# Attention and MoE in one kernel: token rows of eight, one-hot matmuls for the global tokens, bias matmuls for the mask, and units of eight query blocks

## The chip, the cores and the metric

The kernel runs on one core of one Trainium2 chip. The metric is device time in microseconds (us). On one core a run is called slow when it is over 1.5% above the fastest run of the same kernel, and slow runs are left out of every ratio. Ratios below are the mean time of one kernel's fast runs over that of the other's of the same rounds, so they are not quite the ratio of the medians that are quoted.

The kernel before took 381.72 us, the median of three runs (380.2 to 382.25).

## The reference

```python
# batch 8, heads 8, sequence 576, head size 64; 8 global tokens, window 32
def _attn_ref(q, k, v, global_idx):
    scores = scale * np.matmul(q, k.transpose(0, 1, 3, 2))
    mask = np.abs(pos[:, None] - pos[None, :]) <= window
    mask = mask | is_global[:, None] | is_global[None, :]
    scores = np.where(mask, scores, -1000000000.0)
    ...                                   # softmax
    return np.matmul(attn, v)

# 4608 tokens, d_model 512, d_ff 2048
def _moe_ref(x, w_in, w_out, alpha):
    h = x @ w_in
    s = np.sin(alpha * h)
    g = h + s * s / (alpha + 1e-09)
    return g @ w_out
```

A query sees the keys within 32 positions and eight global keys. A global query sees all keys. The result of the attention is the input of the two layers. The comparison with the reference has a tolerance.

## The kernel before

Each batch has 12 blocks of 48 queries for each of four pairs of heads. A block sees 112 window keys and 8 global keys, and its 48 columns of queries are followed by 8 columns of global queries, so a block is 56 columns wide. A unit is six blocks. For each unit the tensor engine (PE) makes scores, ScalarE (ACT) the exponentials, VectorE (DVE) the mask product, PE the denominators and numerators, and DVE writes the result into `xT`, which is the transposed input of the first layer for all 4608 tokens. The matmuls of batch p-1's second layer are laid between the units of batch p's attention as filler, and then batch p's first layer follows.

The start of the kernel gathers the rows of the global tokens of all batches, 24 transfers with offsets that are read at run time, into tiles of their own:

```python
    gN = [setup.tile([NG * B, DM], F32, name=f"gN{i}") for i in range(3)]
    ...
    for i, src in enumerate((k, q, v)):
        for eng, js in halves:
            for j in js:
                eng.dma_start(
                    out=gN[i][j : NG * B : NG, :].rearrange("b (h d) -> b h d", d=D),
                    in_=src[:, :, bass.ds(regs[j], 1), :].rearrange("b h o d -> b h (o d)"),
                )
    ...
    # cast to bf16, transpose, and put into the global columns of qT and kTw,
    # and into the global rows of the value tile by a broadcast transfer:
    globals_all()
    globals_v_all()
    shift_v(0)
    global_v(0)
```

The layers and the tail of the attention:

```python
    # first layer of batch c (512 tokens; nine such, the last without attention ahead of it):
    # a 128-row slice of d_ff at a time
    for ci in range(CT):
        nc.tensor.matmul(out=h2[:], lhsT=w_in[:, ci, nt * P : (nt + 1) * P],
                         rhs=xT[:, ci, c * CH : (c + 1) * CH], ...)
    ...
    # end of a batch's attention: the columns of the eight global queries
    for j in range(NG):
        nc.gpsimd.tensor_copy(
            out=xT[:, :, b * S : (b + 1) * S][:, :, bass.ds(pregs[j], 1)],
            in_=xg[:, :, j : j + 1],
        )
```

The softmax here doesn't subtract the row's maximum and nothing guards it: scores larger than these inputs give would overflow.

## Time and profile before

The span of the profiled run is 378.6 us. I divide it at the starts of the first layers:

| piece of the span | us |
|---|---|
| from the start to the first layer of batch 0 | 46.60 |
| batch-1 period (to the first layer of batch 1) | 43.49 |
| batch-2 period | 38.12 |
| later periods, each | 38.0 |
| from the first layer of batch 2 to the end | 250.4 |

The page's second part shows the span in forty slices. A digit is the busy share of PE in tenths, and PEclk is the clock that was granted to it.

```profile
PE   1127499698999999999999999999999999999996
PEclk9999999999999999999999999999999999999999
```

From the eleventh slice on PE is at nine tenths: the kernel is bound by the tensor engine, except in the first five slices, which are 47 us. The timeline of PE shows what these consist of. The columns are start, duration, engine, source line, operation with output and inputs, shapes, count, and in brackets the idle time ahead of it with what ended it.

```profile
14.44 0.39 PE L268 MATMUL ops<-identb,gB 64*128 64x64 bf16 x4 [6.92 <-DVE gB L266]
...
19.76 0.46 PE L336 MATMUL Sp<-qT,kTw 64*128 64x56 bf16 x12
...
29.58 0.57 PE L375 MATMUL num<-E,VW 128*64 128x56 bf16 x12 [3.08 <-DMA VW<-VgN]
...
42.73 0.52 PE L375 MATMUL num<-E,VW 128*64 128x56 bf16 x12 [0.45 <-DVE gn L386]
46.60 0.59 PE L457 MATMUL hb<-xT,w_in 128*128 128x512 bf16 x1 [3.35 <-POOL xT L402]
...
90.09 9.67 PE L457 MATMUL hb<-xT,w_in 128*128 128x512 bf16 x43 [1.46 <-POOL xT L402]
...
128.21 9.66 PE L457 MATMUL hb<-xT,w_in 128*128 128x512 bf16 x43
```

The start is a chain of waits. The gathered rows come first (14.44), then scores (19.76), then the first numerator waits for the broadcast of the global values (29.58), then eight units follow to 42.73, and the copies on POOL (GpSimd) end the wait for the first layer at 46.60. The difference of two first-layer starts is a period. PE is little loaded up to the first numerator. The windows view gives, for 8 to 30 us, the length and then the busy time of PE, PEld (weight loads), DVE, ACT and POOL, the clock and the load of the DMA engines:

```profile
8.00:30.00 22.00, 4.20 (x72) 3.04 (x72) 11.60 (x37) 5.49 (x8) 14.97 (x22) 1.00 1.70 148
```

PE works for 4.20 of the 22 us. The copy of the keys out of PSUM is a unit-step copy, in the page's fifth part (busy, mean ns):

```profile
L310 DVE COPY kTw<-Kps 128x1344 bf16<-128x1344 bf16 x32 | 27.1, 848 | 1.9 <-PE Kps L304 1.9
```

### The profile page before, as it was taken

To read this page: it belongs to the slowest core of one execution; us is meant where nothing else is said; L and a number is where in the kernel's file an instruction comes from. 1 tells how busy PE (TensorE), PEld (TensorE's weight loads), DVE (VectorE), ACT (ScalarE), POOL (GpSimd) and SP (SyncE) were. 2 spreads that over 40 slices of the span, in tenths; PEclk is the share of its full clock that TensorE was granted. 3 is DMA by queue.
4 is the path that set the end of the run, shared out by engine and by line. 5 is a ranking of instruction groups with operands and counts; after the bars stand their busy time and mean duration, and the time that the engine had idled before them with its cause. 6 is when DMAs were issued, how large, how long until landed. Compare 5 with 4: busy or idle time off the path is not lost.

```text
span 378.6 us, 8594 instructions
## 1 busy us (share of the span) xinstructions
PE 328.3 (87%) x3173; PEld 164.0 (43%) x3224; DVE 244.5 (65%) x556; ACT 258.1 (68%) x435; POOL 245.6 (65%) x390
## 2 busy tenths in 40 slices
PE   1127499698999999999999999999999999999996
PEld 0015244343444444444444444445444544444444
DVE  7735459574987487748774877487748774866510
ACT  1056587795998588858885888588858885845411
POOL 8944297136979489948994899489948303965100
PEclk9999999999999999999999999999999999999999
DMA  6999999546999428951896289628962001000112
GB/s 52 131 167 168 192 156 162 56 51 90 156 135 164 103 40 74 164 109 45 70 165 110 47 64 167 110 51 62 169 100 58 29 32 55 2 1 28 55 57 83
DMA packets 133867, 35.31 MB, mean 93 GB/s; under 512 B 123330, under 2 KB 128450, under 8 KB 133826
## 3 DMA queue, kind: packets, MB, share of 16 engines
q0 software_dynamic: 122560, 19.02, 70.0%
q1 hardware_dynamic: 8034, 15.40, 14.1%
q10 hardware_dynamic: 3232, 0.34, 0.8%
q8 instruction: 25, 0.41, 0.5%
q14 instruction: 16, 0.13, 0.1%
HBM read 38.42 MB, written 9.44 MB: 126 GB/s over the span
## 4 chain that ended last, share of the span: by engine, by line
PE 53%; ACT 17%; POOL 10%; issue 8%; DVE 8%; DMA 2%; POOLq 1%; ACTq 0%; DVEq 0%
PE hb L457 22%; PE ops L494 12%; PE o L494 8%; ACT Sb L464 6%; ACT E L342 3%; PE num L375 3%; ACT S L470 2%; DVE H2b L447 2%; DMA KS<-in_k_dram 2%; DVE S L472 2%; DVE kTw L310 2%; PE hb L494 2%; PE Sp L336 2%; ACT lnd L358 2%; POOL QS L95 2%
## 5 line engine op out<-in xcount | busy, mean ns | idle before, releaser
L457 PE MATMUL hb<-xT,w_in 128*128 128x512 bf16 x562 | 130.7, 382 | 7.0 <-POOL xT L402 4.8
L464 ACT ACTIVATE Sb<-hb,alphaT 128x512 bf16<-128x512 f32 x144 | 96.6, 684 | 52.4 <-PE hb L457 51.1
L447 DVE SCALAR_TENSOR_TENSOR H2b<-S,recipT,hb 128x512 bf16<-128x512 bf16 x144 | 102.2, 740 | 21.0 <-POOL S L472 21.0
L472 POOL TENSOR_TENSOR S<-Sb 128x512 bf16<-128x512 bf16 x87 | 88.4, 1040 | 29.7 <-ACT Sb L464 29.5
L457 PEld LDWEIGHTS <-w_in 128*128 128x128 bf16 x576 | 56.4, 98 | 73.7 <-issue 9.5
L494 PE MATMUL ops<-w_out,H2b 128*128 128x512 bf16 x286 | 73.3, 380 | 2.3 <-issue 1.7
L494 PEld LDWEIGHTS <-H2b 128*128 128x128 bf16 x560 | 48.7, 98 | 52.6 <-issue 2.2
L344 DVE TENSOR_TENSOR E<-E,MASK 128x672 bf16<-128x672 bf16 x64 | 33.1, 519 | 32.8 <-ACT E L342 32.1
L494 PE MATMUL o<-w_out,H2b 128*128 128x512 bf16 x206 | 50.6, 379 | 2.2 <-issue 1.9
L342 ACT ACTIVATE E<-Sp 128x672 bf16<-128x672 f32 x64 | 45.9, 717 | 4.1 <-PE Sp L336 4.0
L402 POOL COPY xT<-xg 128x4 bf16 x64 | 12.9, 201 | 48.7 <-DVE xg L400 45.3
L107 POOL DMA_DIRECT2D VW<-in_v_dram x56 | 42.7, 796 | 0.4 <-issue 0.3
L358 ACT ACTIVATE lnd<-den 128x288 f32<-128x288 f32 x64 | 26.4, 412 | 17.7 <-PE den L352 17.2
L472 DVE TENSOR_TENSOR S<-Sb 128x512 bf16<-128x512 bf16 x35 | 20.4, 582 | 25.0 <-ACT Sb L464 24.1
L382 DVE TENSOR_TENSOR xT<-num,rec 128x288 bf16<-128x288 f32 x64 | 28.7, 448 | 6.8 <-PE num L375 5.4
L375 PEld LDWEIGHTS <-VW 128*64 128x64 bf16 x768 | 18.3, 116 | 32.6 <-DVE gn L386 10.2
L375 PE MATMUL num<-E,VW 128*64 128x56 bf16 x768 | 25.3, 201 | 6.6 <-DMA VW<-VgN 3.1
L360 ACT ACTIVATE rec<-lnd 128x288 f32<-128x288 f32 x64 | 28.3, 443 | 2.0
L310 DVE COPY kTw<-Kps 128x1344 bf16<-128x1344 bf16 x32 | 27.1, 848 | 1.9 <-PE Kps L304 1.9
L336 PE MATMUL Sp<-qT,kTw 64*128 64x56 bf16 x768 | 22.1, 190 | 6.0 <-ACT E L342 4.2
L100 POOL DMA_DIRECT2D QS<-in_q_dram x30 | 23.6, 786 | 2.8 <-DMA QS<-in_q_dram 2.8
L324 ACT COPY qT<-qp 128x576 bf16<-128x576 bf16 x20 | 12.6, 632 | 18.1 <-DMA gN<-in_v_dram 13.7
(77 smaller groups left out, 314.3 us busy)
## 6 DMA issues: line engine op xcount, KB each, us to landing
out_dram<-osb SPq DMA_DIRECT2D x35, 256.0 KB
VW<-in_v_dram POOLq DMA_DIRECT2D x40, 112.0 KB, 4.4
VW<-VW SPq DMA_DIRECT2D x8, 384.0 KB
KS<-in_k_dram POOLq DMA_DIRECT2D x30, 96.0 KB, 4.6
QS<-in_q_dram POOLq DMA_DIRECT2D x30, 96.0 KB, 4.6
w_in<-in_moe_w_in_dram POOLq DMA_DIRECT2D x4, 512.0 KB, 9.0
w_out<-in_moe_w_out_dram POOLq DMA_DIRECT2D x4, 512.0 KB, 13.7
VW<-VW SPq DMA_DIRECT2D x8, 240.0 KB
```

The costliest lines, as they stand in the source:

```text
L107: nc.gpsimd.dma_start(out=W[p0 : p0 + n, par, u, :].rearrange("p (h d) -> p h d", d=D), in_=v[b, :, key0 : key0 + n, :].rearrange("h p d - ...
L310: nc.vector.tensor_copy(out=kTw[hp][:, :, 0:KB], in_=bass.AP(tensor=base.tensor, offset=base.offset, ap=[list(base.ap[0]), [QB, NW], [1, KB]],
L336: nc.tensor.matmul(out=Sp[:, t, u * QC : (u + 1) * QC], lhsT=kTw[hp][pr, i, :], rhs=qT[hp][pr, i, :], start=True, stop=True, skip_group_ch ...
L342: nc.scalar.activation(out=E[:], in_=Sp[:, :, 0:EW], func=AF.Exp, scale=scale)
L344: nc.vector.tensor_tensor(out=E[:], in0=E[:], in1=mk[:, None, :].to_broadcast([P, 2, EW]), op=ALU.mult)
L358: nc.scalar.activation(out=lnd[:], in_=den[:, :, 0:QB], func=AF.Ln)
L375: nc.tensor.matmul(out=num[pr, u, :], lhsT=W[:, i % 2, i // 2, c0 : c0 + 64], rhs=E[:, t, u * QC : (u + 1) * QC], start=True, stop=True, s ...
L447: nc.vector.scalar_tensor_tensor(out=H2b[:, n_, :], in0=s_[:], scalar=recipT[:, n_ : n_ + 1], in1=h_, op0=ALU.mult, op1=ALU.add,)
L457: nc.tensor.matmul(out=h2[:], lhsT=w_in[:, ci, nt * P : (nt + 1) * P], rhs=xT[:, ci, c * CH : (c + 1) * CH], start=(ci == 0), stop=(ci == ...
L464: nc.scalar.activation(out=Sb[:], in_=h2[:], func=AF.Sin, scale=alphaT[:, nt : nt + 1])
L472: eng.tensor_tensor(out=S2[:], in0=Sb[:], in1=Sb[:], op=ALU.mult)
L494: nc.tensor.matmul(out=ops[:], lhsT=H2b[:, nt, ts * P : (ts + 1) * P], rhs=w_out[:, nt, :], start=(nt == 0), stop=(nt == NT - 1),)
```

## The change

The intent is to start without the gathers. For batches 0 and 1, q and k come in rows of eight tokens. The global rows of q, k and v of these two batches are picked by matmuls with one-hot matrices that the core makes from the indices. Batch 0 gets its mask as a bias, added to the scores by a matmul with the identity, so that ACT's exponentials are masked already. The 24 gathers are still needed for batches 2 and later, and are moved behind the start: twelve are issued after the first shift of v, twelve inside the first layer of batch 0. Their rows are put into a part of `xT` that the attention does not fill until batch 6. The one-hot matrices lie in another such part, that of batches 4 and 5. The unit becomes eight blocks, so there are six units per batch.

The diff, cut to its core (the address arithmetic of the transposes, the mask tables and the renamed arguments are left out):

```diff
+    NB = 8
...
+    late_x = slice(NTOK - 2 * DM, NTOK)
+    gN = [xT[0 : NG * B, i, late_x].bitcast(F32) for i in range(3)]
+    gB = [xT[0 : NG * B, 3, NTOK - (2 - i) * DM : NTOK - (1 - i) * DM] for i in range(2)]
...
-    gN = [setup.tile([NG * B, DM], F32, name=f"gN{i}") for i in range(3)]
-    halves = ((nc.sync, range(0, NG // 2)), (nc.scalar, range(NG // 2, NG)))
-    ...                                   # all 24 gathers in the setup
...
+    OHV = xT[:, 0, early_x : early_x + (NU + 1) * P].rearrange("p (a b) -> p a b", b=P)
+    VgZ = xT[:, 1, early_x : early_x + DM]
...
+    def globals_v(b):                     # global rows of v by one-hot matmuls
+        for u in range(NU):
+            nc.tensor.matmul(
+                out=vp[:], lhsT=OHV[0:KB, u, :], rhs=W[0:KB, 0, u, :], ...
+            )
+        ...
+        nc.vector.tensor_copy(out=VgZ, in_=vp[:])
...
+    def globals_hp(b, hp, pool, tag):     # global rows of q and k by one-hot matmuls
+        for i, src in enumerate((qk[b][1], qk[b][0])):
+            for j in range(R8):
+                for t, pr in heads:
+                    nc.tensor.matmul(
+                        out=gp[pr, i, :],
+                        lhsT=src[:, 2 * hp + t, j, :], rhs=OH[0:NP8, j, :], ...
+                    )
...
+        if b == 0:                        # the mask of batch 0
+            for t, pr in heads:
+                nc.tensor.matmul(
+                    out=Sp[:, t, 0:EW], lhsT=identb[:],
+                    rhs=BIAS[:, i0 : i0 + NB, :].rearrange("p u c -> p (u c)"),
+                    start=True, stop=False, ...
+                )
...
-            nc.gpsimd.tensor_copy(
+            copy, r = nc.gpsimd.tensor_copy, pregs
+            if b == 0 and j % 2:
+                copy, r = nc.scalar.copy, aregs
+            copy(
...
+        if b == 2 and hp == 0:
+            zero(Kps[:, 0:WIN].bitcast(F32))
+            zero(Kps[:, WIN + S : WIN + S + WIN].bitcast(F32))
...
+    def start_sync():
+        shift_v(0)
+        gathers.extend(gather_all())
+        for f in gathers[:12]:
+            f()
...
+        ... Q(4), partial(globals_v, 0), V(0), D_(3), Q(5), V(1), alpha_in, D_(4), ...
...
+                    fill = mm2(0, H2[0], ((psC, "ops"), (psA, "o2")) * 2)
+                    fill[2:2] = [fill.pop(4), fill.pop(4)]
+                    counts = [1, 1, 2, 3, 3, 3, 2, 1, 0]
...
+                if p == 0:                # inside the first layer of batch 0
+                    pre[1:1] = [partial(globals_v, 1)]
+                    pre += gathers[12:]
```

## The prediction

> **What bounds it now.** Steady batches are bound by the tensor engine. In the timeline the first-layer matmuls of successive batches start at 90.1, 128.2, 166.3, 204.2 us: 38.0 apart, engine shares at 9 tenths (page, part 2). Of 38.0, the two layers take 2 x 64 x 0.216 = 27.6, transposes 2.1, scores 8 x 0.26, denominators 8 x 0.25, numerators 8 x 0.21; under 2 us are real gaps. The start is not: the first layer of batch 0 starts at 46.6 us, with the tensor engine busy 16 us until then (windows). In order of time: head loads land at 6.0; gathered global rows are there by 15.6; masks and globals done 17.8; an activation-table load; first exp at 21.8; the first numerator waits for the broadcast of global v until 29.6; eight units follow 1.9 apart; last numerator 42.7; then a tail of 3.9, of which 2.03 are eight one-column copies on GpSimd. Batch 1 costs 43.5 instead of 38.0: ACT does half the squares (0.63 each) and k/q arrive late.
>
> **The change.** Removed from the start: the wait for 24 gathers, the affine selects on GpSimd, one table load (1.28), six mask multiplies (0.5 each), the wait for the v broadcast, four of eight tail copies on GpSimd (1.0). Loads of k, q of batches 0 and 1 become fewer, longer rows.
> Added for batch 0: bias matmuls (2 x 448 columns a unit), v-global matmuls, seven 512-column one-hot matmuls, and per head pair 32 transposes and 32 one-hot matmuls instead of 12 transposes. The tensor engine is slow there: 12 score matmuls take 0.46 against 0.33 later. The Trainium skill (TensorE: Matmul & The Clock Gate, Part 1) gives half clock until about 3.4 us of sustained work; the trace agrees, still slow at 42 us. Estimate: up to 29 us of slow tensor work, so this engine becomes a second limit of the start. The k copy reads PSUM with a stride; the skill (VectorE: DVE Perf Modes, What auto-detection actually checks) wants step 1 for the double rate, which today's 0.85 us for 1344 elements shows; estimate 1.5.
> Units: six of 448 columns instead of eight of 336. Tensor work is nearly unchanged; ACT goes from 8 x 1.5 to about 6 x 1.8 us a batch, off the critical path: it can only shrink gaps.
>
> **On the critical path.** First exp near 10.5 (-11), but transposes, bias and one-hot matmuls give part back: first numerator 25 to 29, then steps of 1.8 (single numerator buffer: matmuls, multiply, reduce). First layer of batch 0 starts at 37.5 (34 to 42): -9. Batch 1: squares off ACT and no late loads save 4, one-hot and split transposes plus v globals cost 3.5: period 43, -0.5. Six steady periods of 37.5: -3. The rest unchanged.
>
> **Prediction: 369 us, 8 in 10 within 360 to 377. Faster by over 2%: 0.78; within 2%: 0.19; slower: 0.03.**
>
> **What would show it.** First exp at 10 to 12 us; first-layer start of batch 0 at 34 to 42; batch-1 period 42 to 44; steady periods 37 to 38; strided k copy near 1.5 us on DVE; batch 0's score matmuls still slow; no wait for gathers before the first exp.
>
> **What would make it wrong.** The tensor engine warm from 15 us on: start at 33, total 363. w_in, w_out or batch-1 rows late (about 9 MB must land by 54 us instead of 62): a stall around 50 us. Longer exps making single-buffered scores wait in steady steps: periods of 38.5, total 375. Gaps in steady batches all vanish (36.5): below 363.

## The result, and the profile after

The changed kernel took 427.63 us, the median of four runs (423.3 to 429.75, the slowest of them slow), against 381.99 for the kernel before. The ratio of the fast runs is 1.117, with a 95% interval from 1.107 to 1.126. It is slower by about 12%. The profiled run, with a span of 426.3 us, was fast.

| piece of the span, us | before | after | difference |
|---|---|---|---|
| start to the first layer of batch 0 | 46.60 | 59.99 | +13.4 |
| batch-1 period | 43.49 | 71.60 | +28.1 |
| batch-2 period | 38.12 | 44.92 | +6.8 |
| first layer of batch 2 to the end | 250.4 | 249.8 | -0.6 |

All of the loss is in the first 177 us. The forty slices of the page show two holes in PE's work, in slices three and four and again in slice eight, and a lowered clock in the second and behind it:

```profile
PE   2832759068886799999999899999989989999996
PEclk9999999576898789999999999999999999999999
```

The timeline of PE after:

```profile
11.44 0.56 PE L525 MATMUL Sp<-qT,kTw 64*128 64x56 bf16 x16
...
40.30 2.72 PE L349 MATMUL ops<-VW,xT 112*128 112x512 bf16 x6 [14.00 <-DMA xT<-in_q_dram]
...
43.48 0.63 PE L577 MATMUL num<-E,VW 112*64 112x56 bf16 x16
...
55.67 0.63 PE L577 MATMUL num<-E,VW 112*64 112x56 bf16 x16 [0.85 <-DVE gn L543]
...
59.99 0.58 PE L681 MATMUL hb<-xT,w_in 128*128 128x512 bf16 x1 [3.31 <-ACT xT L615]
...
86.69 0.61 PE L681 MATMUL hb<-xT,w_in 128*128 128x512 bf16 x1 [12.95 <-DMA xT<-in_v_dram]
...
131.59 11.05 PE L681 MATMUL hb<-xT,w_in 128*128 128x512 bf16 x43 [3.82 <-POOL xT L615]
...
176.51 9.66 PE L681 MATMUL hb<-xT,w_in 128*128 128x512 bf16 x43
```

The scores are there at 11.44 instead of 19.76, as intended. But the one-hot matmuls for v (L349) then wait 14.00 us, and the first layer of batch 0 stops in its middle for 12.95 us. Both waits end with a transfer into `xT` from q or v in memory, and the only such transfers are the gathers. The queue of the sync engine shows when they are issued (start, time for the group of issues):

```profile
23.27 6.30 SPq L366 DMA_DIRECT2D xT<-in_k_dram  x8
29.76 4.23 SPq L366 DMA_DIRECT2D xT<-in_q_dram  x4
...
75.83 3.09 SPq L366 DMA_DIRECT2D xT<-in_q_dram  x4
79.11 6.10 SPq L366 DMA_DIRECT2D xT<-in_v_dram  x8
```

PE's waits end 6.3 and 1.5 us after the last issue of the two pairs of groups. Yet the waiting instructions do not need the gathered rows. L349 reads the one-hot matrices in columns from 2560 on of `xT`, and the first layer of batch 0 reads columns 0 to 511, while the gathers write columns 3584 to 4607 in the first 64 partitions. The casts that first use these rows are at 122.9 us in this trace. The list of semaphore waits in the program as built has these two instructions wait for all eight lanes of the hardware transfers (a lane is a counter by which the program follows its transfers).

Other readings answer to the prediction. The first exponential starts at 12.03 us on ACT, in the timeline:

```profile
12.03 0.92 ACT L531 ACTIVATE E<-Sp 128x896 bf16<-128x896 f32 x1 [2.09 <-PE Sp L525]
```

The copy of the keys with a stride takes 1.55 us on DVE, against 0.85 for the unit-step copy of the same number of elements:

```profile
23.33 1.55 DVE L439 COPY kTw<-o 128x1344 bf16<-128x1344 bf16 x1
```

The Trainium skill (VectorE: DVE Perf Modes, What auto-detection actually checks) asks for 16-bit operands of step 1 for the doubled rate, and the two durations agree with it.

The lowered clock is seen in the windows: 0.59 from 74.0 to 86.7 us, which is the second hole itself, and a mean of 0.84 from there to the first layer of batch 1 (86.7 to 131.6). The Trainium skill (TensorE: Matmul & The Clock Gate, Part 1) says that an idle window of about 3.4 us puts the clock to half, and that about as long a busy window brings it back. This trace agrees for holes: after the 3.82 us ahead of batch 1's first layer, 43 matmuls take 11.05 us, and without a hole 9.66 (both lines above). A hole costs more than its length.

### The profile page after: what moved, and what is told of

Its sections match the earlier page's. It is cut to its first block, busy times and chain, and to the rows that moved or that the text cites. A ratio compares the mean times of both kernels' runs of the same rounds, so it can differ in the third digit from the quotient of the medians.

```text
span 426.3 us, 9332 instructions
## 1 busy us (share of the span) xinstructions
PE 351.2 (82%) x3598; PEld 176.0 (41%) x3653; DVE 241.6 (57%) x522; ACT 247.7 (58%) x378; POOL 244.6 (57%) x369
## 4 chain that ended last, share of the span: by engine, by line
PE 51%; issue 15%; ACT 11%; POOL 8%; DVE 7%; DMA 7%; POOLq 1%; ACTq 0%; DVEq 0%
PE hb L681 24%; PE ops L718 10%; PE o L718 8%; DMA VW<-in_v_dram 5%; ACT E L531 3%; ACT Sb L688 2%; DVE S L696 2%; POOL S L696 2%; PE num L577 2%; DVE H2b L671 2%; DVE kTw L480 2%; DMA QS<-in_q_dram 2%; PE hb L718 2%; ACT L632 2%; ACT rec L566 1%
## 5 line engine op out<-in xcount | busy, mean ns | idle before, releaser
L696 POOL TENSOR_TENSOR S<-Sb 128x512 bf16<-128x512 bf16 x111 | 112.9, 1040 | 63.5 <-ACT Sb L688 62.5
L531 ACT ACTIVATE E<-Sp 128x896 bf16<-128x896 f32 x48 | 43.6, 909 | 14.3 <-PE Sp L525 14.3
L564 ACT ACTIVATE lnd<-den 128x384 f32<-128x384 f32 x48 | 23.5, 490 | 46.6 <-PE den L558 46.6
L535 DVE TENSOR_TENSOR E<-E,MASK 128x896 bf16<-128x896 bf16 x42 | 26.2, 625 | 31.1 <-ACT E L531 31.0
L596 DVE TENSOR_TENSOR xT<-num,rec 128x384 bf16<-128x384 f32 (+1 forms) x64 | 27.5, 451 | 21.2 <-PE num L577 16.4
L131 POOL DMA_DIRECT2D KS<-in_k_dram x36 | 28.2, 784 | 0.0
L525 PEld LDWEIGHTS <-kTw 64*128 64x128 bf16 x768 | 16.0, 97 | 27.2 <-issue 19.2
L577 PEld LDWEIGHTS <-VW 120*64 120x64 bf16 (+1 forms) x768 | 17.1, 117 | 21.6 <-issue 10.4
L566 ACT ACTIVATE rec<-lnd 128x384 f32<-128x384 f32 x48 | 25.1, 523 | 1.5
L577 PE MATMUL num<-E,VW 120*64 120x56 bf16 (+1 forms) x768 | 22.2, 200 | 1.8 <-DVE gn L549 1.0
```

What stands on the lines that cost most here:

```text
L131: nc.gpsimd.dma_start(out=dst[:, t, :, :], in_=src[b, :, t * TW : (t + 1) * TW, :].rearrange("h p d -> p h d"),)
L525: nc.tensor.matmul(out=Sp[:, t, m * QC : (m + 1) * QC], lhsT=kTw[hp][pr, i, :], rhs=qT[hp][pr, i, :], start=b > 0, stop=True, skip_group_c ...
L531: nc.scalar.activation(out=E[:], in_=Sp[:, :, 0:EW], func=AF.Exp, scale=scale)
L566: nc.scalar.activation(out=rec[:], in_=lnd[:], func=AF.Exp, scale=-1.0)
L577: nc.tensor.matmul(out=num[pr, m, :], lhsT=W[0:nk, i % 2, i // 2, c0 : c0 + 64], rhs=E[0:nk, t, m * QC : (m + 1) * QC], start=b > 0 or m = ...
L596: nc.vector.tensor_tensor(out=xT[:, hp, x0 : x0 + nb * QB].rearrange("p (u c) -> p u c", u=nb), in0=num[:, m0 : m0 + nb, 0:QB], in1=rec[:, ...
```

## The experiments

Theory A was that the gathers stall everything that reads `xT`, because their rows were parked in it. Theory B was the rival that the prediction had also named as a danger: the transfers of weights and rows are late, whatever tile the gathers go to. Further questions were whether larger units help the steady batches (C, no; D, yes), and what the remaining loss in batch 1 was: placement of the filler (E) or the added tensor work (F).

| run | median us | ratio to before | start | batch 1 | batch 2 | rest |
|---|---|---|---|---|---|---|
| before (profile) | 381.99 | | 46.60 | 43.49 | 38.12 | 250.4 |
| after | 427.63 | 1.117 | 59.99 | 71.60 | 44.92 | 249.8 |
| early_gathers | 411.22 | 1.077 | 56.85 | 58.21 | 45.16 | 249.8 |
| setup_gathers | 399.03 | 1.047 | 47.24 | 54.85 | 43.91 | 249.2 |
| units_only | 380.31 | 0.996 | 45.10 | 46.45 | 38.33 | 250.2 |
| fill_back | 388.70 | 1.020 | 46.00 | 49.40 | 40.70 | 249.1 |
| fill_zero | 384.50 | 1.002 | 47.06 | 49.18 | 37.97 | 249.1 |
| mended | 383.38 | 1.003 | 47.76 | 46.45 | 37.99 | 249.2 |
| mended2 | 382.71 | 1.003 | 46.52 | 46.62 | 37.99 | 249.1 |
| own_slots_control | 429.47 | 1.125 | 60.83 | 71.78 | 44.94 | 251.7 |
| own_slots | 402.24 | 1.056 | 46.85 | 56.55 | 44.80 | 251.6 |

The four right columns are from the profiled run of each, cut as above, and add up to its span. The first three experiments ran on one chip, the next three on another, and so on, each call with the kernel before beside it.

### early_gathers: all gathers issued at once, still into `xT`

```diff
     def start_sync():
-        shift_v(0)
         gathers.extend(gather_all())
-        for f in gathers[:12]:
+        for f in gathers:
             f()
+        shift_v(0)
...
-                    pre += gathers[12:]
```

> Edit: in the changed kernel all 24 gathers of global rows are issued together, ahead of the shift of v of batch 0; they still write into the unused end of xT. Theory A (false wait: the gathers write xT, so the next instruction on each engine that touches any part of xT waits for all of them): the 13 us stall in the middle of the first layer of batch 0 is gone, because no gather is issued after it; the 14 us stall before the one-hot v matmuls of batch 0 shrinks to the time at which 24 gathers land, about 25 to 30 us instead of 40. First layer of batch 0 starts at 46 to 50 us (after: 60.0), batch-1 period 50 to 58 (after: 71.6), time 392 to 408 us. Rival B (v loads and their shift are late because the DMA queues are full): the wait before the one-hot v matmuls stays until about 40 us or later, since the shift is issued even later; time 412 to 425.

It took 411.22 us (410.26 to 411.76), above the range that theory A gave; the first layer started at 56.85 us, where A had 46 to 50. In the timeline of PE the wait inside the first layer is gone, and the one in front of the one-hot matmuls is 9.94 us and ends with the last gathers:

```profile
36.49 2.72 PE L349 MATMUL ops<-VW,xT 112*128 112x512 bf16 x6 [9.94 <-DMA xT<-in_v_dram]
```

The wait moved with the gathers, as A says, but these landed later than I expected, at 36 us instead of 25 to 30: their issue alone lasts until 31 us. A is supported. B is not excluded, because the shift of v moved too.

### setup_gathers: all gathers into tiles of the setup

```diff
-    gN = [xT[0 : NG * B, i, late_x].bitcast(F32) for i in range(3)]
-    gB = [xT[0 : NG * B, 3, NTOK - (2 - i) * DM : NTOK - (1 - i) * DM] for i in range(2)]
...
     setup = tc.alloc_tile_pool(name="setup", bufs=1)
+    gN = [setup.tile([NG * B, DM], F32, name=f"gN{i}") for i in range(3)]
+    gB = [setup.tile([NG * B, DM], BF, name=f"gB{i}") for i in range(2)]
...
-        for f in gathers[:12]:
+        for f in gathers:
...
-        pool_regs, V(3), V(4), V(5), last0,
+        pool_regs, V(3), V(4), V(5), last0, partial(globals_all, psC, "ops"),
...
-                        (6, [partial(globals_all, psA, "qp"), partial(globals_in, 2, 0), ...
+                        (6, [partial(globals_in, 2, 0), ...
...
-                    pre += gathers[12:]
```

> Edit: the gathered rows go to tiles of their own instead of the end of xT, all 24 gathers are issued where the first 12 stood (after the shift of v), and they are turned into GT and VgN at the end of the attention of batch 0. Theory A (false wait through xT): both stalls (14.0 and 13.0 us in the trace) are gone although the gathers still land at 40 us or later; the one-hot v matmuls of batch 0 start at 26 to 28 us (after: 40.3), first layer of batch 0 at 45 to 49 us (after: 60.0), batch-1 period 48 to 58 (after: 71.6), time 388 to 404 us. Rival B (v or the DMA queues late): the one-hot v matmuls still wait until about 40 us, time 412 or more. In both cases the kernel should not beat the kernel before if the rest of the start gains nothing.

It took 399.03 us (396.97 to 399.88), and both waits are gone. In the timelines of PE and DVE the one-hot matmuls start at 27.07 although the gathers land only near 45, where the cast of the rows waits for them:

```profile
27.07 2.74 PE L349 MATMUL ops<-VW,xT 112*128 112x512 bf16 x6
...
44.95 0.82 DVE L376 CAST gB<-gN 64x512 bf16<-64x512 f32 x2 [0.18 <-DMA gN<-in_v_dram]
```

So the v rows and the weights were not what PE waited for, and B falls. What is left is a gap of 3.49 us ahead of batch 1's scores, one of 3.84 ahead of its first layer, and one of 3.04 for a memset in batch 2:

```profile
70.80 0.38 PE L525 MATMUL Sp<-qT,kTw 64*128 64x56 bf16 x16 [3.49 <-DVE H2b L671]
...
102.09 11.34 PE L681 MATMUL hb<-xT,w_in 128*128 128x512 bf16 x44 [3.84 <-POOL xT L615]
116.47 0.64 PE L474 MATMUL Kps<-identb,KS 96*128 96x96 bf16 x6 [3.04 <-DVE Kps L191]
```

### own_slots and its control: the same issues at the same place, another tile

setup_gathers moved work as well as the rows. The purest test needs 4 KB per partition more than is free, so the control gives up a buffer in two pools:

```diff
-            spool = ctx.enter_context(tc.tile_pool(name="spool", bufs=4))
-            osbp = ctx.enter_context(tc.tile_pool(name="osbp", bufs=2))
+            spool = ctx.enter_context(tc.tile_pool(name="spool", bufs=3))
+            osbp = ctx.enter_context(tc.tile_pool(name="osbp", bufs=1))
```

> The changed kernel with one buffer fewer for the squares of the first layer (3 for 4) and one for the output rows (1 for 2), which is the memory that the next run needs; nothing else. Theory A (the waits for the gathers are all that the start is longer by): the two waits of the tensor engine, 14.0 and 13.0 us, stand as in the changed kernel; first layer of batch 0 at 59 to 61 us. The fewer buffers cost whatever they cost in every batch, 0 to 10 us in all.

own_slots is this control with

```diff
-    gN = [xT[0 : NG * B, i, late_x].bitcast(F32) for i in range(3)]
+    gOwn = const.tile([NG * B, 2, DM], F32, name="gOwn")
+    gN = [gOwn[:, i % 2, :] for i in range(3)]
```

> The control, with the gathered rows in a tile of their own; every instruction stands where it stood. The tile has two slots for three sets of rows, so the values of v lie over those of k, and the global keys of batches 2 and later are wrong on purpose. Theory A (readers of the first layer's input tile wait for gathers because these write into that tile): the tensor engine's waits of 14.0 and 13.0 us before the one-hot v matmuls and inside the first layer are gone though the gathers land when they did; one-hot v matmuls at 26 to 28 us, first layer of batch 0 at 47 to 50 us, batch-1 period down by 12 to 17 us, time 23 to 30 us under the control's. Rival B (transfers of the v rows, weights and gathers, queued one behind the other, come late whatever tile they go to): the waits stay within 3 us of the control's, under the name of another transfer, and the time within 6 us.

The control took 429.47 us (428.0 to 430.96), with waits of 14.72 and 13.05 us. own_slots took 402.24 us (400.32 to 404.96), 27.2 less by the medians. Its global keys of batches 2 and later are wrong on purpose; the comparison does not guard these keys, and I did not test why. The control, and below it own_slots, in the timelines of PE and of the sync engine's queue:

```profile
41.12 2.72 PE L349 MATMUL ops<-VW,xT 112*128 112x512 bf16 x6 [14.72 <-DMA xT<-in_q_dram]
...
87.70 4.40 PE L681 MATMUL hb<-xT,w_in 128*128 128x512 bf16 x12 [13.05 <-DMA xT<-in_v_dram]
...
23.55 6.31 SPq L366 DMA_DIRECT2D xT<-in_k_dram  x8
```

```profile
25.94 2.74 PE L350 MATMUL ops<-VW,xT 112*128 112x512 bf16 x6
...
29.15 0.63 PE L578 MATMUL num<-E,VW 112*64 112x56 bf16 x16
...
41.15 0.63 PE L578 MATMUL num<-E,VW 112*64 112x56 bf16 x16 [0.85 <-DVE gn L544]
...
60.84 2.76 PE L682 MATMUL hb<-xT,w_in 128*128 128x512 bf16 x12
...
23.86 6.31 SPq L367 DMA_DIRECT2D gOwn<-in_k_dram  x8
```

The gathers are issued at the same time, 23.86 against 23.55, but the one-hot matmuls run at 25.94 instead of 41.12, and the first layer goes on without its stop. The start is shorter by 14.0 us and the batch-1 period by 15.2. This settles A: parking the rows in `xT` costs 27 of the 46 us lost. What the pair does not settle is why the waits are there though the regions don't overlap. The list of waits in the program as built says more, in builds that were not run on the chip. In own_slots the two instructions wait for none of the lanes. In the changed kernel with one edit, eight rows next to each other (`j * B : (j + 1) * B`) as the target of a gather in place of every eighth row (`j : NG * B : NG`), they wait for none either, though the rows still go into `xT`. With the offsets of the gathers fixed instead of read at run time the waits stay. So in this program it is the step of eight rows in the target that makes a gather count against readers of other parts of the tile, and not the shared tile as such. The time of that build was not measured.

own_slots also shows the start without that stall, and it is no shorter than before: 46.85 against 46.60 us. In the windows view PE now works 18.08 of the 22 us from 8 to 30:

```profile
8.00:30.00 22.00, 18.08 (x311) 10.61 (x311) 9.36 (x28) 11.02 (x16) 10.88 (x15) 1.00 1.38 182
```

### units_only: the larger units alone, in the kernel before

The edit takes over the eight-block units with their buffers and nothing else:

```diff
+    NB = 8
...
-    EW = NU * QC
+    EW = NB * QC
...
-    units = [(hp, hf) for hp in range(NHP) for hf in range(2)]
-    NUN = len(units)
...
-                    counts = [1] * NP_
-                    counts[-1] = 0
+                    counts = [1, 1, 1, 1, 1, 2, 2, 1, 0]
```

> Edit: only the 8-block units (six of 448 columns instead of eight of 336), with their step counts, put into the kernel before; loads, gathers, masks, transposes as before. My prediction said 37.5 us a steady batch (-0.5 each). Theory C (the steady batch is bound by the tensor engine, whose matmuls stay the same, so longer units change nothing): steady period 37.9 to 38.1, start 1 to 4 us earlier than 46.6 because fewer serial steps run in batch 0, time 376 to 382 us. Rival D (longer single-buffered scores stall the tensor engine, or gaps shrink): period off 38.0 by 0.4 or more, time under 375 or over 384.

It took 380.31 us (379.99 to 381.83), a ratio of 0.9964 with an interval from 0.9944 to 0.9984. The steady periods are 37.98 us, where they were 38.0. The larger units save 1.5 us at the start and lose 3.0 in batch 1. C holds: the steady periods did not get shorter, so ACT's saved time was not on the critical path there, and the gaps that I hoped to shrink did not shrink. The prediction gave them 3 us.

### fill_back and fill_zero: batch 1's filler and a memset

fill_back starts from setup_gathers, and lays batch 0's second layer between the units of batch 1 as the other batches do:

```diff
-                    fill[2:2] = [fill.pop(4), fill.pop(4)]
+                    fill.pop(0)()
+                    fill.pop(0)()
-                    counts = [1, 1, 2, 3, 3, 3, 2, 1, 0]
+                    counts = [1, 1, 1, 1, 1, 2, 2, 1, 0]
```

> Edit on top of setup_gathers: in batch 1 the second-layer matmuls of batch 0 are placed as in every later batch, two slots ahead of the first scores and four slots after the last numerators, instead of none ahead, none after and three a step. Theory E (with no matmuls at hand the tensor engine idles 3.5 us before the first scores of batch 1 and 3.8 us before its first layer, and after each such gap runs at about half rate for some us): both gaps close to under 1.5 us in sum and batch 1 shrinks by more than the gaps, period 54.9 to 44 to 48 us, time 399 to 387 to 393 us. Rival F (the extra tensor work of one-hot and split transposes is what batch 1 costs, the gaps are only where it waits): period falls by 3 us or less, time 396 or more.

It took 388.7 us (387.02 to 393.07, the slowest slow). The batch-1 period fell by 5.45 us and the batch-2 period by 3.2. That is more than the gaps themselves shrank, because the half rate behind them went too, as the 44 first-layer matmuls of batch 1 and the next line show:

```profile
71.18 0.38 PE L525 MATMUL Sp<-qT,kTw 64*128 64x56 bf16 x16 [1.81 <-DVE H2b L671]
...
95.40 9.66 PE L681 MATMUL hb<-xT,w_in 128*128 128x512 bf16 x44
```

They took 11.34 us in setup_gathers. E holds in kind, and its time came true, but the period of 49.40 us is above its 44 to 48, and one gap of 1.81 us is left, where it had under 1.5 in sum. F falls as the main cause: the added one-hot and split transposes were still there. The placement was not all gain: in this run and the next the first layer of batch 0 waits 1.9 us for DVE, which it does not in setup_gathers.

fill_zero is fill_back with the two edge memsets of `Kps` moved from batch 2's transposes into batch 1's attention:

```diff
-        if b == 2 and hp == 0:
-            zero(Kps[:, 0:WIN].bitcast(F32))
-            zero(Kps[:, WIN + S : WIN + S + WIN].bitcast(F32))
...
+                    parts[4] = partial(chain, parts[4],
+                        partial(zero, Kps[:, 0:WIN].bitcast(F32)),
+                        partial(zero, Kps[:, WIN + S : WIN + S + WIN].bitcast(F32)))
```

> Edit on top of fill_back: the two memsets that clear the edges of Kps for the row layout of batch 2 are issued during the attention of batch 1, after the last copy of its k, instead of right before the transposes of batch 2. Theory E: the 3.0 us wait of the transposes for the vector engine's queue in the first layer of batch 1 goes, and with it the slow matmuls behind it; the period of batch 2 falls from 43.9 (or what fill_back leaves) to 38.0 to 39.5 us, time 1.5 to 5 us below fill_back, 383 to 390 us. Rival F: the time stays within 1 us of fill_back.

It took 384.5 us (381.05 to 385.05). The 3.04 us wait is gone, and the batch-2 period is 37.97 us, the steady one.

### mended and mended2: the start

mended is fill_zero with alpha's split moved ahead of the units that it stalled, and with all eight tail copies of batch 0 on GpSimd:

```diff
-            if b == 0 and j % 2:
-                copy, r = nc.scalar.copy, aregs
...
-        Q(3), D_(2), masks,
+        Q(3), alpha_parts, D_(2), masks,
...
-        ... V(1), alpha_in, D_(4), ...
+        ... V(1), D_(4), alpha_in, ...
```

> Edits on top of fill_zero: all eight column copies of batch 0 back on GpSimd (in the trace the four on ScalarE and four on GpSimd took turns, 2.05 us for all, as long as the eight on GpSimd alone before), and the split of alpha into three bf16 parts moved from the middle of the numerators (2.4 us in the vector engine's queue) to an idle stretch of that engine earlier. Expected: the tail copies take 2.0 us as before, no gain; the start shortens by 1.5 to 2.5 us through alpha; first layer of batch 0 at 44.5 to 46 us; time 381 to 388 us. If the copies had overlapped on two engines, the start would get about 1 us longer for that part.

It took 383.38 us (382.82 to 384.87). The eight copies take 2.05 us on GpSimd alone, and took 1.95 (45.06 to 47.01) when they alternated with ACT in fill_zero, so the second engine had overlapped almost nothing. The timeline of fill_zero names the reason, each copy waits for the one before it on the other engine:

```profile
45.29 0.21 ACT L612 COPY xT<-xg 128x4 bf16 x1 [4.03 <-POOL xT L612]
...
45.56 0.20 POOL L612 COPY xT<-xg 128x4 bf16 x1 [0.30 <-ACT xT L612]
```

The last numerator came 2.8 us sooner (39.95 instead of 42.73), but the start did not shorten: it is 47.76 us, where I expected 44.5 to 46. In the timelines of DVE and POOL a cast waits for the gathers until 45.04, and the profile puts the copies' wait down to it. The third line, of the view by source line, shows another reason. It is the loads of the eight column offsets into GpSimd's registers, with the shortest, median and longest in ns and the first and last start:

```profile
45.04 0.42 DVE L379 CAST gB<-gN 64x512 bf16<-64x512 f32 x1 [2.23 <-DMA gN<-in_v_dram]
...
45.66 2.05 POOL L613 COPY xT<-xg 128x4 bf16 x8 [4.51 <-DVE gB L379]
...
L415 POOLq TENSOR_LOAD <-gsc x8: 285/289/497, 40.2 to 44.6; - x8
```

These loads stand behind the last weight transfer in GpSimd's order and just ahead of the copies. They and the register steps after each run until 45.1, and the profile does not count them as busy. The data of the copies were ready at 42.21, and in the program as built the first copy waits for that data alone, so the loads held the copies, and not the cast. In the kernel before the same loads were over by 30.3 us.

mended2 issues half of the gathers ahead of the shift of v:

```diff
+    regs = [nc.sync.value_load(...) for j in range(NG)]     # at the start
...
-        shift_v(0)
-        for f in gathers:
+        for f in gathers[:12]:
+            f()
+        shift_v(0)
+        for f in gathers[12:]:
             f()
```

> The mended kernel, with the first twelve gathers of the global rows issued ahead of the query part's shift of the first 64 rows and the other twelve right behind it. Theory (the casts gB wait for the last gathers, which land at 45.0 us and hold the tail of batch 0): gathers land by 38 us, the casts wait for none, the first layer of batch 0 starts at 44 to 46 us (47.76 in mended), batch-1 period 44 to 46.5, steady period 38.0, time 378 to 382. Rival (the shift of the first rows, behind twelve gathers in the queue, now comes later and with it the first one-hot matmuls): one-hot v matmuls start 2 us or more later than in mended, first layer at 47 us or later, time 383 or more.

It took 382.71 us, the median of six (380.27 to 384.08), a ratio of 1.0027 with an interval from 0.999 to 1.0065. The casts no longer wait for the gathers, and the one-hot matmuls were not later (25.90 instead of 26.33), so the rival falls. But the start is 46.52 us, above the 44 to 46 that I expected, and the time is 0.7 us above its range too. The timeline of POOL, and the offset loads again:

```profile
44.42 2.05 POOL L613 COPY xT<-xg 128x4 bf16 x8 [5.63 <-DVE VgN L389]
...
L415 POOLq TENSOR_LOAD <-gsc x8: 286/296/1190, 37.9 to 43.3; - x8
```

The copies begin at 44.42, though their data were ready at 41.85. The profile names a cast of the gathered v rows, which ends at 44.06, but in the program as built the first copy does not wait for it. The offset loads end at 43.9, just before the copies, so the theory was wrong on what held them. The start shortened by 1.2 us because the weight transfer ahead of the loads was issued 2.35 us sooner (37.90 instead of 40.25). No run moved the loads themselves; by the 2.6 us between 41.85 and 44.42 I estimate that doing so would take about 2 us off the start. No version beat the kernel before by more than the 0.4% of units_only.

## Why the prediction was wrong

The prediction was 369 us, and the result 427.63 us.

**"Removed from the start: the wait for 24 gathers."** This is the step that failed. The gathers were not removed but moved, and parked in every eighth row of a corner of `xT`, which nearly everything reads. The wait moved to the one-hot matmuls (14.0 us) and into the first layer (12.95 us). own_slots removes 27.2 us against its control by changing the tile alone. I had compared the order of the instructions on each engine before and after, and the order shows nothing of this. The waits of the program as built show it, and I had not read them.

**"First layer of batch 0 starts at 37.5: -9."** Without the stall it would still have started at 46.85 us (own_slots). The first part of the mechanism was right: the first exponential came at 12.03 us, where the text had 10.5 and a range to 12. The later terms were mis-sized. The first numerator comes at 29.15, where I had 25 to 29. From it to the last one are 12.0 us, where five steps of 1.8 make 9.0: the last three steps are 1.6 to 2.0, but the first two are 3.1 and 3.5, with alpha's split in the second. From the last numerator to the first layer are 5.7 us, where I had taken the 3.9 of before less 1.0. The 1.0 for "four of eight tail copies" was 0, as mended showed, and about 1.4 us more are the offset loads on GpSimd, which the change had moved to just before these copies: the copies' data were ready at 43.41, and the first began at 44.84. The idea that the tensor engine "becomes a second limit of the start" was right and undervalued: 18.08 of 22 us busy in place of 4.20, so the wait for the gathers was exchanged for tensor work of about the same length.

**"Period 43, -0.5" for batch 1.** It was 71.60 us. Of the 28.1 us more, the shared tile accounts for 15.2 by own_slots, the half rate behind the hole included. From setup_gathers to fill_back the filler's placement took 5.45 away. From fill_zero to mended a further 2.7 went; the 1.92 us wait for DVE in batch 0's first layer is gone in mended, and whether the moved split of alpha brings this about was not tested. Of the rest, 1.7 lie between own_slots and setup_gathers. The 3.0 us that remain against the kernel before are found in units_only as well, which has none of the one-hot work but a schedule of its own for batch 1. In mended, the one-hot matmuls for v take 1.7 us and the split transposes with their one-hot matmuls about 4.7, in place of 2.1 of plain transposes, so the added tensor work is about 4.3 us, where the text had 3.5. How much of the 3.0 is that work and how much is schedule, I did not settle.

**Batch 2** was not in the prediction as a piece of its own. Its 6.8 us are the filler of batch 1 with its half rate (3.2), and the memset (2.7), and the rest is in the difference between the kernels that these were measured in.

**"Six steady periods of 37.5: -3."** They stayed at 38.0, in the changed kernel and in units_only.

**"w_in, w_out or batch-1 rows late: a stall around 50 us."** There was a stall, and the text gave a chance of 3% to a slower kernel. But the cause named was not the one: setup_gathers ran without the stall with the same loads.

**"Strided k copy near 1.5 us"** (1.55) and **"batch 0's score matmuls still slow"** (0.56 for 16 at 11.44, and 0.38 for the same 16 in batch 1 in fill_back) were right.

## What to carry to other kernels

An unused corner of a large tile is not free memory: a slow transfer into it can hold up readers of its other parts, here for 14 and 13 us, and by the builds it hung on the row step of the transfer's target. So look at the waits of the built program and not only at the order of its instructions. Work that moves off a chain has to be costed on the engine that takes it: here the wait for gathers became tensor work of about the same length. Steps that the profile does not count as busy, such as the register loads on GpSimd, can still be on the chain, so read the order of an engine's instructions where its wait seems to have no owner. Gaps of 3 to 4 us on the tensor engine cost more than they last, so filler belongs where the gaps are.

## What the Trainium skill lacked or had wrong

- No page that I read says that a transfer into one region of a tile can make instructions wait that read other regions of it. It cost 14.0 and 12.95 us in the changed kernel, and 27.2 us by the pair of own_slots and its control. It comes from the waits in the program as built, not from the chip.
- TensorE: Matmul & The Clock Gate, Part 1, says that about 3.4 us of sustained work bring the full clock. In own_slots PE was busy for 18.08 of the 22 us from 8 to 30 us, and the groups were still slow: six 512-column one-hot matmuls took 2.74 us at 25.94, and the same six took 1.46 us at 58.01 in the same run. The recorded clock for 8 to 30 us was 1.00, so the records don't show this half rate. How busy is busy enough, the runs don't settle.
- The same page puts the idle window for the half clock at about 3.4 us. The runs show nothing against it, only a price: a gap of 3.8 us cost 1.4 to 2.8 us in the 43 or 44 matmuls behind it (11.05 in the changed kernel, 11.34 in setup_gathers, 12.05 in own_slots and 12.46 in early_gathers instead of 9.66 us), and the filler's placement took 8.7 us from two periods, of which its gaps were 5.5 (3.49 and 3.84 down to 1.81).
- No page that I read says that copies to column offsets read at run time may not overlap across two engines when they write one tile: eight took 1.95 us alternating between GpSimd and ACT in fill_zero, and 2.05 on GpSimd alone in mended. The wait is the program's: as built, each copy has a semaphore wait for the one before it on the other engine.
